# One kernel, another sequence of its work list: logits of the first unit first, unit 2 ahead of the queries, the first projection ahead of a mixing product

## The chip, the cores and the metric

The kernel runs on 1 core of one Trainium2 chip. The metric is the device time of one execution in microseconds; lower is better. The core has five engines with queues of their own: PE (TensorE, matrix products), DVE (VectorE), ACT (ScalarE), POOL (GpSimd) and SP, which here only issues DMA transfers. Each engine runs its own instructions strictly in the order in which the program lists them and waits for semaphores of the others.

## The reference

Four tensors q, k, v and f_logit of shape (4, 8, 768, 48) go through a gated linear recurrence, and its result through a Fourier mixing layer with a two-layer network (768 tokens, 384 channels, 1536 hidden channels):

```python
f = 1.0 / (1.0 + np.exp(-f_logit))
for t in range(S):
    state = f[:, :, t, :, None] * state + np.einsum('bhd,bhe->bhde', k[:, :, t], v[:, :, t])
    y[:, :, t] = np.einsum('bhd,bhde->bhe', q[:, :, t], state)
# x: y as (4, 768, 384)
X = np.fft.fft(np.fft.fft(x, axis=1), axis=2)
u = x + np.real(X)
un = (u - mean(u)) / np.sqrt(var(u) + 1e-06)
return u + np.maximum(un @ w_ch1, 0.0) @ w_ch2
```

## The kernel before, in words

The recurrence is cut into 16 **units**: unit u is batch u // 4 and a pair of heads (u % 4). A unit's channels lie on the partitions and its 768 tokens along the free axis, in six chunks of 128 tokens. The Fourier layer is a product with tables over tokens and one over channels, done per batch once its four units are there. The network is done per batch in three pairs of 128-token blocks.

Each unit is a Python generator (`attention` and `outputs`), and one `next` runs it to its next `yield`. A batch has three more generators: `fnet` (the Fourier products), `turns` (normalising and transposing for the network) and `projected` (the network). What runs when is written out by hand in one string, `ORDER`, of 970 words. Each word makes one step, and the loop behind it at line 1074 and following records the instructions of that step at once. So the sequence of the words is the sequence on every engine. There is no scheduler behind it. A word `L2fk` issues the loads of logits and keys of unit 2 on SP, a bare number such as `2` runs the next step of unit 2, `K2` transposes its weighted keys, `F0`, `H0`, `P0` step the three generators of batch 0, `r` loads a block of network weights (they come in 64-bit words) and `C` converts a loaded block to 32 bits, `I` sets constants, `i` loads the identity matrix, `E` prepares the triangle of ones for the running sums, `Z` clears buffers.

The lines that the steps below speak of:

- Line 411 (ACT) takes exp(-logits) in place. For the four units of batch 0, PE then transposes it by chunks into PSUM (423, tiles `pg`), ACT takes the logarithm out of PSUM (425, into `early`), PE forms the running sums with the triangle (433, `run`), and ACT makes the two weights out of them (439, 440) and the ends (441). For later units DVE does the running sums with a scan (449) instead.
- Lines 462 and 464 (DVE) multiply queries and keys by the weights, in place. 472 (PE, `sc`) forms the token-by-token products, 476 (DVE) copies the allowed half to SBUF (`at`), 610 (PE, `st`) transposes the weighted keys, 631 and 648 (PE) form the outputs and the second half of the products, 673 (PE, `ds`) the state increments, 681 (DVE, `stt`) scans the states, 690 (PE) adds their share to the output.
- Lines 319, 321, 322, 323 convert a block of weights (ACT, DVE twice, POOL).
- Line 824 (PE, `mix`) is the channel product of the Fourier layer, 883 (DVE) adds its result to x, 865 (PE, `pt`) transposes normalised rows, 959 (PE, `up`) is the first layer of the network for the first two block pairs. Later pairs use a scheme with 15 products instead of 24 whose sums DVE makes (899) for PE (927).
- PSUM: the tiles named `run`, `sc`, `st`, `ds`, `yt` share two buffers in turn, the tiles `pg`, `z`, `mix`, `pt`, `up` share two others. A step that takes a buffer waits until its earlier content has been read.
- The program gives SP's transfers eight semaphores in turn, so a further one is issued when the one eight places before it has landed. A load into a buffer also waits for the last reader of what lay there; the keys of units 0 and 3 share one buffer (`k_87` in the lists below).

Of the kernel before, what the change touches and what calls it, by code (L numbers as in the profile page):

```python
# [12 lines left out]
C = 128  # L13
# [11 lines left out]


ORDER = (
# [27 lines left out]
)  # L55


# [1162 lines left out]
```

## Time and profile before

| what | us |
|---|---|
| median of three runs | 508.57 (508.08 to 509.59) |
| the profiled execution's own time | 512.57 |
| its span, first to last instruction | 510.8 |
| PE busy in the span | 485.5 (95%) |
| DVE busy | 363.8 (71%) |
| ACT busy | 233.1 (46%) |
| POOL busy | 89.5 (18%) |
| mean granted clock of PE | 0.993 |

Busy time of PE counts a matrix product from its start to its modelled end. Products overlap, so a busy PE need not be at its peak. In a timeline row, the first number is the start in us from the start of the span, the second the duration, and the bracket at the end says how long the engine sat idle before and what ended that. The profiled execution took 4.0 us more than the median of the unprofiled runs.

### The profile page before, as it was taken

The page shows a single profiled execution, that of the slowest core. Times are in us where ns is not written, and L with a number is a line of the kernel's source. Part 1 is how long each engine was busy: PE and PEld are TensorE (multiplying, and loading weights), DVE is VectorE, ACT ScalarE, POOL GpSimd, SP SyncE. Part 2 cuts the span into 40 slices and gives each one's busy share as a digit, 9 for nine tenths or more (in the row PEclk, how much of TensorE's full clock was granted, in tenths as well). Part 3 has the DMA queues.
Part 4 walks back from the last instruction along what each step waited for, and adds up shares of the span by engine and source line. Part 5 has one row for each costly group of instructions (what it writes and reads, how often), then busy time and mean ns, then how long its engine had stood idle before and what let it go on. Part 6 is the DMA issues. An engine that isn't in the chain of part 4 may idle for free.

```text
span 510.8 us, 13829 instructions
## 1 busy us (share of the span) xinstructions
PE 485.5 (95%) x5806; PEld 450.2 (88%) x5806; DVE 363.8 (71%) x711; ACT 233.1 (46%) x552; POOL 89.5 (18%) x136
## 2 busy tenths in 40 slices
PE   4878889999999999999999999999999999999997
PEld 4766677886798999998998989999999999999997
DVE  2489988999959684585777886777486666558653
ACT  4688678866230541446463554452431413232130
POOL 2126632644222100000031000111000000010100
PEclk9799999999999999999999999999999999999999
DMA  8877946555201101113011112121200331134001
GB/s 225 236 210 192 248 144 206 170 174 155 83 1 47 38 3 37 43 54 103 30 48 37 49 43 59 58 57 41 98 1 15 110 124 63 62 138 143 31 3 38
DMA packets 20075, 46.20 MB, mean 90 GB/s; under 512 B 3489, under 2 KB 6242, under 8 KB 20002
## 3 DMA queue, kind: packets, MB, share of 16 engines
q1 hardware_dynamic: 18898, 41.66, 28.0%
q0 software_dynamic: 1104, 3.54, 1.9%
q8 instruction: 48, 0.79, 0.7%
q14 instruction: 25, 0.20, 0.1%
HBM read 40.47 MB, written 4.72 MB: 88 GB/s over the span
## 4 chain that ended last, share of the span: by engine, by line
PE 87%; DVE 4%; DMA 3%; ACT 2%; issue 2%; POOL 1%; SPq 0%; POOLq 0%; DVEq 0%; ACTq 0%
PE ub L927 26%; PE fx L982 17%; PE fz L982 12%; PE up L959 6%; PE y L631 3%; PE z L804 3%; PE po L968 3%; PE mix L824 2%; PE y L690 2%; PE ds L673 2%; PE sc L472 2%; PE pt L865 2%; DMA raw<-in_w_ch_dram 2%; PE yt L711 1%; PE run L433 1%
## 5 line engine op out<-in xcount | busy, mean ns | idle before, releaser
L936 DVE TENSOR_TENSOR h<-h,ub 128x512 f32<-128x512 f32 x90 | 61.0, 686 | 32.4 <-PE ub L927 24.7
L934 ACT ACTIVATE h<-ub 128x512 f32<-128x512 f32 x60 | 35.6, 593 | 51.9 <-PE ub L927 50.6
L772 POOL DMA_INDIRECT out_dram<-x,place x16 | 21.3, 1332 | 179.8 <-DVE x L1040 124.3
L927 PE MATMUL ub<-wide,w 128*128 128x128 f32 x400 | 49.8, 276 | 1.7 <-DVE wide L899 1.7
L927 PEld LDWEIGHTS ub<-wide,w 128*128 128x128 f32 x400 | 47.3, 192 | 2.4 <-DVE wide L899 1.6
L939 ACT ACTIVATE h<-h 128x512 f32<-128x512 f32 x50 | 31.1, 632 | 35.2 <-DVE h L936 35.2
L982 PE MATMUL fx<-block,h 128*128 128x192 f32 x264 | 46.7, 327 | 0.0
L982 PE MATMUL fx<-w,h 128*128 128x192 f32 x264 | 45.6, 328 | 0.0
L982 PEld LDWEIGHTS fx<-block,h 128*128 128x128 f32 x264 | 43.4, 190 | 0.2
L982 PEld LDWEIGHTS fx<-w,h 128*128 128x128 f32 x264 | 42.6, 190 | 0.2
L927 PE MATMUL ub<-unT,w 128*128 128x128 f32 x320 | 41.0, 275 | 0.0
L927 PEld LDWEIGHTS ub<-unT,w 128*128 128x128 f32 x320 | 38.4, 192 | 0.0
L323 POOL TENSOR_TENSOR w<-w,raw 128x384 uint32<-128x384 uint32 x24 | 27.7, 1161 | 56.7 <-ACT raw L319 18.7
L959 PE MATMUL up<-unT,w 128*128 128x256 f32 x144 | 33.2, 384 | 0.1
L927 PE MATMUL ub<-wide 128*128 128x128 f32 x240 | 31.9, 276 | 0.9 <-DVE wide L899 0.9
L927 PE MATMUL ub<-unT,wide 128*128 128x128 f32 x240 | 32.2, 277 | 0.0
L866 ACT COPY unT<-pt 128x384 f32<-128x384 f32 x24 | 11.4, 476 | 42.2 <-PE pt L865 42.0
L959 PEld LDWEIGHTS up<-unT,w 128*128 128x128 f32 x144 | 26.7, 190 | 4.3 <-DVE x L887 0.4
L927 PEld LDWEIGHTS ub<-wide 128*128 128x128 f32 x240 | 29.4, 192 | 1.2 <-PE ub L927 1.1
L927 PEld LDWEIGHTS ub<-unT,wide 128*128 128x128 f32 x240 | 29.2, 192 | 0.4
L982 PE MATMUL fz<-block,h 128*128 128x192 f32 x132 | 23.5, 328 | 0.0
L476 DVE COPY_PREDICATED at<-causal,sc 128x768 f32<-128x768 uint32 x16 | 16.6, 1040 | 9.3 <-PE sc L472 8.0
(216 smaller groups left out, 1011.4 us busy)
## 6 DMA issues: line engine op xcount, KB each, us to landing
raw<-in_w_ch_dram SPq DMA_DIRECT2D x24, 384.0 KB, 5.1
v<-in_v_dram SPq DMA_DIRECT2D x16, 288.0 KB, 3.8
k<-in_w_ch_dram SPq DMA_DIRECT2D x12, 384.0 KB, 3.6
g<-in_w_ch_dram SPq DMA_DIRECT2D x12, 384.0 KB, 4.1
k<-in_qkf_dram SPq DMA_DIRECT2D x25, 144.0 KB, 3.4
g<-in_qkf_dram SPq DMA_DIRECT2D x20, 144.0 KB, 4.6
q<-in_qkf_dram SPq DMA_DIRECT2D x20, 144.0 KB
wide<-in_qkf_dram SPq DMA_DIRECT2D x11, 144.0 KB, 4.3
```

What stands on the lines that cost most here:

```text
L323: nc.gpsimd.tensor_tensor(bits, bits, lo, ALU.add)
L476: nc.vector.copy_predicated(AT, causal[:, :64].bitcast(U32).unsqueeze(1).unsqueeze(1).to_broadcast([128, 2, NCH, 64]), own[:, :, :NCH * 64 ...
L631: nc.tensor.matmul(y[FILL[g], c // 3, c % 3 * C + t.start:c % 3 * C + t.stop], lhsT=vals[rows, o:o + (64 if g == 0 else D)], rhs=weights, ...
L772: nc.gpsimd.indirect_dma_start(out=out.rearrange("b s d -> (b s) d"), out_offset=bass.IndirectOffsetOnAxis(ap=place[:, b, i:i + 1], axis=0 ...
L804: nc.tensor.matmul(z[:, cols], lhsT=src[:, j, lo:hi], rhs=tab[:, t, T % 2, cols], start=(i == 0), stop=(i == len(parts) - 1), skip_group_c ...
L927: nc.tensor.matmul(chains[chain][:, m * 128:(m + 1) * 128], lhsT=block(w)[:, m * 128:(m + 1) * 128], rhs=tokens(a), start=(new and m == 0) ...
L934: nc.scalar.activation(out, got, kind, scale=1.0 if how == "=+" else -1.0)
L936: nc.vector.tensor_tensor(out, out, got, ALU.add if how == "+" else ALU.subtract)
L939: nc.scalar.activation(out, out, AF.Relu)
L959: nc.tensor.matmul(pp[:, :256], lhsT=w1[:, kt, m * 128:(m + 1) * 128], rhs=unT[:, kt], start=(kt == 0), stop=(kt == 2))
L968: nc.tensor.matmul(po[:, :DM], lhsT=h[:, m, t], rhs=w2[:, m], start=(m == 0), stop=(m == NF - 1))
L982: nc.tensor.matmul(out, lhsT=h[:, m], rhs=blocks[i][:, m], start=(start and m == 0), stop=(m == H - 1), skip_group_check=True)
```

## The change

Only the string `ORDER` differs. Both hold the same 970 words, each the same number of times, so the same instructions are recorded, in another sequence. (Where buffers are handed out in turn, the tile numbers differ.) The start of the diff:

```diff
 ORDER = (
-    "I L1f L0f i L0v E 1 0 0 1 0 0 L0k r C 0 1 1 0 L0q 0 0 1 L2f 2 L1q 0 Z 0 K0 0 0 r 2 2 r 1 L1k 1 L3fk "
-    "L2q 0 0 2 1 0 0 1 3 1 L2k C C 2 L1v 0 3 3 K1 L4fk 0 1 0 2 L3q 3 1 1 1 2 2 4 1 0 1 3 3 3 L3v 1 2 3 2 "
+    "Z E L0f 0 L1f 1 i L2f r L0q L0v L0k 0 L2k 2 I 1 r 0 0 C 0 2 1 1 0 0 0 1 L1q 1 0 2 0 K0 0 2 L3fk 1 "
+    "L1k 0 0 0 3 1 2 0 K1 3 3 L2q 0 0 2 1 L3v 2 1 L1v C 1 1 L4fk L3q 0 2 0 0 0 3 1 1 1 3 3 3 L2v 3 1 4 2 "
...
```

The rest of the string differs all along, by small moves: the first `P0` stands at place 216 instead of 220, units 8 and 9 change places for a while, the last 31 words are `P3` in both.

**First place: the loads at the start, on SP.** `g_85`, `k_87`, `q_89` and `v` are logits, keys, queries and values of unit 0, `g_86` and `q_90` logits and queries of unit 1, `raw` a block of weights; the first `wide` is the logits of unit 2. Before:

```order
L250 DMA g_86<-in_qkf_dram 96x768
L251 DMA g_86<-in_qkf_dram 16x768
L250 DMA g_85<-in_qkf_dram 96x768
L251 DMA g_85<-in_qkf_dram 16x768
L1112 DMA ident<-in_ident_dram 128x128
L233 DMA v_141<-in_v_dram 128x576
L234 DMA vx_142<-in_v_dram 64x288
L244 DMA k_87<-in_qkf_dram 48x768
L246 DMA k_87<-in_qkf_dram 32x768
L248 DMA k_87<-in_qkf_dram 16x768
L348 DMA raw_176<-in_w_ch_dram 128x768
L250 DMA q_89<-in_qkf_dram 96x768
```

Now:

```order
L250 DMA g_85<-in_qkf_dram 96x768
L251 DMA g_85<-in_qkf_dram 16x768
L250 DMA g_86<-in_qkf_dram 96x768
L251 DMA g_86<-in_qkf_dram 16x768
L1112 DMA ident<-in_ident_dram 128x128
L250 DMA wide<-in_qkf_dram 96x768
L251 DMA wide<-in_qkf_dram 16x768
L348 DMA raw_144<-in_w_ch_dram 128x768
L250 DMA q_89<-in_qkf_dram 96x768
L251 DMA q_89<-in_qkf_dram 16x768
L233 DMA v_148<-in_v_dram 128x576
L234 DMA vx_149<-in_v_dram 64x288
```

The logits of unit 0 are loaded ahead of those of unit 1, and those of unit 2 follow at once; values and keys of unit 0 come later. Further on, the keys of unit 1 stand behind the keys of units 2 and 3, where they stood ahead of both.

**Second place: DVE around units 1 and 2.** `q_90`, `g_86` are unit 1's, `stt_351` and `stt_355` unit 0's states, `at_92` unit 1's products, `wide` in lines 462 and 464 is unit 2's. Before:

```order
L462 TENSOR_TENSOR q_90<-q_90,g_86 112x768
L464 TENSOR_TENSOR g_86<-W_202,k_88 112x768
L681 SCALAR_TENSOR_TENSOR stt_351<-ds_332,te_98 112x288
L476 COPY_PREDICATED at_92<-causal,sc_0_363 128x768
L321 TENSOR_SCALAR w_107<-raw_282 128x384
L322 SCALAR_TENSOR_TENSOR w_107<-raw_282,w_107 128x384
L321 TENSOR_SCALAR w_107<-raw_294 128x384
L322 SCALAR_TENSOR_TENSOR w_107<-raw_294,w_107 128x384
L462 TENSOR_TENSOR wide<-wide 112x768
L464 TENSOR_TENSOR wide<-W_401,wide 112x768
```

Now:

```order
L462 TENSOR_TENSOR q_90<-q_90,g_86 112x768
L464 TENSOR_TENSOR g_86<-W_227,k_88 112x768
L681 SCALAR_TENSOR_TENSOR stt_355<-ds_338,te_98 112x288
L462 TENSOR_TENSOR wide<-wide 112x768
L476 COPY_PREDICATED at_92<-causal,sc_0_394 128x768
L321 TENSOR_SCALAR w_107<-raw_186 128x384
L322 SCALAR_TENSOR_TENSOR w_107<-raw_186,w_107 128x384
L464 TENSOR_TENSOR wide<-W_351,wide 112x768
```

The query product of unit 2 stands ahead of the copy of unit 1, and one of the two weight conversions there is made later. Ahead of the first line 883 DVE now has 6 conversions, where it had 7; between the first and the second line 883 it has 3 conversions, where it had 2, and a copy (476) that stood there now comes behind.

**Third place: PE at the first projection.** `pt_3` is the transposition that completes its input, `yt` and `y` belong to outputs of units of batch 1, `mix_2` the third mixing product of batch 0. Before:

```order
L865 MATMUL pt_3_1447<-ident,un_3_1397 128x128 x3
L711 MATMUL yt_1460<-ident,yT_1240 128x112 x6
L690 MATMUL y<-wide,stt_1445 48x128 x10
L824 MATMUL mix_2_1477<-cd,zz_1081 128x193 x2
L824 MATMUL mix_2_1477<-cd,zz_1081 128x192 x2
L959 MATMUL up_0_0_1499<-unT_0_1309,w_107 128x256 x3
```

Now:

```order
L865 MATMUL pt_3_1407<-ident,un_3_1368 128x128 x3
L472 MATMUL sc_0_1432<-wide 64x64 x24
L690 MATMUL y<-wide,stt_1416 48x128 x10
L711 MATMUL yt_1479<-ident,yT_1214 128x112 x6
L959 MATMUL up_0_0_1487<-unT_0_1307,w_107 128x256 x3
L824 MATMUL mix_2_1492<-cd,zz_1092 128x193 x2
```

The first projection stands ahead of the third mixing product, no longer behind it.

50 rows, old and new, of the table ORDER are left out of this document.

## The prediction

> **What bounds the kernel now.** I read the page first, for the engine that ends last.
>
> ```profile
> PE 485.5 (95%) x5806; PEld 450.2 (88%) x5806; DVE 363.8 (71%) x711; ACT 233.1 (46%) x552; POOL 89.5 (18%) x136
> ...
> PE   4878889999999999999999999999999999999997
> ...
> PE 87%; DVE 4%; DMA 3%; ACT 2%; issue 2%; POOL 1%; SPq 0%; POOLq 0%; DVEq 0%; ACTq 0%
> ```
>
> PE is the bound: 95% busy, 87% of the chain that ended last, and its slices are full from the eighth on. Since both lists hold the same instructions, PE's work is the same. The time can only move by PE's idle time (510.8 - 485.5 = 25.3 us) and by the rate at which PE runs. Where does the idle time lie? Busy time by stretches of 10 us (PE, PEld, DVE, ACT, POOL, then PE's granted clock, DMA share, GB/s):
>
> ```profile
> 0.00:10.00 10.00, 2.81 (x14) 2.58 (x15) 2.09 (x3) 4.58 (x8) 2.96 (x21) 1.00 0.78 216
> 10.00:20.00 10.00, 8.54 (x128) 7.64 (x127) 5.67 (x7) 6.75 (x13) 3.29 (x12) 0.84 1.04 264
> 20.00:30.00 10.00, 9.48 (x218) 8.30 (x216) 3.77 (x6) 7.89 (x22) 0.98 (x1) 0.82 0.80 219
> 30.00:40.00 10.00, 7.77 (x307) 7.00 (x297) 9.35 (x11) 7.62 (x19) 1.86 (x3) 1.00 0.70 199
> 40.00:50.00 10.00, 7.72 (x237) 6.42 (x230) 9.78 (x17) 8.22 (x20) 6.71 (x12) 1.00 0.70 196
> 50.00:60.00 10.00, 8.41 (x238) 6.81 (x230) 9.44 (x20) 6.54 (x20) 8.75 (x15) 1.00 0.85 219
> 60.00:70.00 10.00, 7.80 (x163) 6.02 (x162) 8.99 (x13) 7.60 (x22) 2.79 (x3) 1.00 0.81 236
> 70.00:80.00 10.00, 8.71 (x224) 7.34 (x225) 8.54 (x19) 8.00 (x26) 2.97 (x3) 1.00 0.52 166
> 80.00:90.00 10.00, 9.54 (x196) 7.71 (x187) 8.53 (x21) 8.46 (x24) 3.74 (x4) 1.00 0.57 175
> 90.00:100.00 10.00, 10.00 (x121) 8.55 (x118) 9.66 (x13) 8.66 (x23) 6.69 (x6) 1.00 0.60 176
> ```
>
> Up to 90 us PE idles 90 - 70.8 = 19.2 us. So 6.1 us are left behind that. From 30 to 60 us DVE is the fullest engine (28.6 of 30 us) and PE waits on it. Up to 30 us DVE has 18.5 us to spare, because it waits for the first loads, logarithms and products. So there are three regimes: a start set by loads and a chain across engines, a middle set by DVE, and from the first projections (85 us) on a PE that always has work. Who ends PE's waits, over the whole span (us in total, times, longest):
>
> ```profile
> PE pg L423 <- ACT g L411: 7.2, 1, 7.2
> PE y L690 <- DVE stt L681: 4.7, 6, 1.3
> PE ub L927 <- DVE wide L899: 2.6, 4, 0.9
> ```
>
> The first is the start, the second the middle, the third all that DVE costs PE in the late stage.
>
> **The change, part by part.** The start, in order of time:
>
> ```profile
> 4.25 0.84 ACT L411 ACTIVATE g<-g 112x768 f32<-112x768 f32 x1 [2.15 <-DMA g<-in_qkf_dram]
> ...
> 4.99 0.19 ACT L411 ACTIVATION_READ_ACCUMULATOR g<-g 112x1 f32 x1
> ...
> 6.20 0.84 ACT L411 ACTIVATE g<-g 112x768 f32<-112x768 f32 x1 [1.01 <-DMA g<-in_qkf_dram]
> ...
> 7.18 2.28 PE L423 MATMUL pg<-ident,g 112*128 112x112 f32 x10 [7.18 <-ACT g L411]
> ...
> 10.89 0.65 ACT L319 ACTIVATE raw<-raw,two 128x384 f32<-128x384 uint32 x1 [1.04 <-DMA raw<-in_w_ch_dram]
> ...
> 12.12 0.90 ACT L439 ACTIVATE g<-run,rise 112x768 f32<-112x768 f32 x1 [0.57 <-PE run L433]
> ...
> 13.05 0.96 DVE L462 TENSOR_TENSOR q<-q,g 112x768 f32<-112x768 f32 x1 [1.27 <-ACT g L439]
> ...
> 14.20 0.96 DVE L464 TENSOR_TENSOR g<-W,k 112x768 f32<-112x768 f32 x1 [0.19 <-DVE q L462]
> ...
> 15.19 0.31 SPq L244 DMA_DIRECT2D k<-in_qkf_dram  x1
> ...
> 16.32 1.04 DVE L476 COPY_PREDICATED at<-causal,sc 128x768 f32<-128x768 uint32 x1 [1.16 <-PE sc L472]
> ...
> 16.90 1.20 PE L610 MATMUL st<-ident,g 112*128 112x112 f32 x5 [0.71 <-ACT deep L441]
> ...
> 18.64 0.96 DVE L464 TENSOR_TENSOR g<-W,k 112x768 f32<-112x768 f32 x1 [0.45 <-DMA k<-in_qkf_dram]
> ...
> 23.78 0.76 DVE L681 TENSOR_TENSOR_SCAN stt<-ds,te 112x288 f32<-112x288 f32 x1 [4.18 <-PE ds L673]
> ...
> 25.32 0.90 ACT L439 ACTIVATE wide<-run,rise 112x768 f32<-112x768 f32 x1 [1.72 <-PE run L433]
> ```
>
> *The first logits.* PE's first products need unit 0's exponentials, which came second (6.20 + 0.84, PE at 7.18). Loaded first they are made at 4.25. PE then waits for the identity, 64 KB behind both pairs of logits, which were there at 6.20.
>
> For landings I use a line through two rows. The first weight block, behind 1768 KB in the old list (by the shapes in the list, itself included), was there at 10.89. Unit 1's keys, behind 3832 KB, were there at 18.64. So 2064 KB took 7.75 us, 0.375 us per 100 KB. The identity lands at about 6.4, and PE starts 0.8 us sooner.
>
> *What takes this gain away.* ACT now also has unit 2's exponential (0.84 + 0.19) between the logarithms, so line 439 of unit 0 starts at about 11.4, not 12.12. Unit 0's keys stand behind 2440 KB, where 1384 KB were, and land at 10.89 + 672 x 0.00375 = 13.4. So line 464 starts at 13.4, 0.8 us sooner, and the copy 476 of unit 0 likewise. But the transposition at line 610 waits for a buffer that unit 1's line 441 frees (0.71 us in the row at 16.90), and unit 1's lines 439 to 441 now stand behind one more logarithm of unit 2 on ACT. I put them where they were. The 0.8 us end there: nil at 17 us.
>
> *Unit 2's running sums* go ahead of unit 0's remaining outputs on PE, so that its line 439 comes well ahead of 25.32. Six of these products delay unit 0's state increments, and the scan at 23.78 moves later. Against that, the increments no longer stand behind other transpositions of unit 2. I take +0.4 us (bounds 0 and +1.5).
>
> *DVE's middle.* The rows that carry it:
>
> ```profile
> 26.91 1.04 DVE L476 COPY_PREDICATED at<-causal,sc 128x768 f32<-128x768 uint32 x1 [2.37 <-PE sc L472]
> 27.84 0.35 DVE L321 TENSOR_SCALAR w<-raw 128x384 uint32<-128x384 uint32 x1
> 28.23 0.56 DVE L322 SCALAR_TENSOR_TENSOR w<-raw,w 128x384 uint32<-128x384 uint32 x1
> ...
> 30.38 0.95 DVE L462 TENSOR_TENSOR wide<-wide 112x768 f32<-112x768 f32 x1
> ...
> 74.52 0.54 DVE L883 TENSOR_TENSOR x<-mix,x 128x384 f32<-128x384 f32 x1
> ```
>
> Ahead of the copy at 26.91 DVE idles 2.37 us, and from there to 74.52 it hardly idles at all. Unit 2's query product (0.95 us at 30.38) now goes into that idle time. It needs unit 2's queries, behind 4696 KB: 18.64 + 864 x 0.00375 = 21.9, early enough. That is -0.95 us. One weight conversion fewer stands ahead of the first line 883: 0.35 + 0.56 = -0.9 us. With +0.4 from the scan, line 883 comes at 74.52 - 1.45, about 73.1. Bounds: 0 if PE, not DVE, holds the middle, and -2.9 if the scan is not late and a second conversion's worth of idle goes.
>
> *The first projection.* Between the first and second line 883 a conversion more (+0.9) and a copy less (-1.04) nearly cancel. PE's order there has the third mixing product behind the projection:
>
> ```profile
> 75.60 1.49 PE L824 MATMUL mix<-cd,zz 97*128 97x193 f32 x8
> ...
> 84.97 1.56 PE L959 MATMUL up<-unT,w 128*128 128x256 f32 x6
> ```
>
> So the first projection comes at 84.97 - 1.5 - 1.5 = 82.0. Only one of these 1.5 us is a gain: the mixing product is done later instead, at its full 1.5. The postponed conversion falls where PE is 10.00 of 10 busy and DVE 9.66, so projections cover it. Without that cover it would cost 0.9.
>
> *The late stage* is shuffled too, by small moves. Its price is PE's wait for DVE's sums, 2.6 us in four pieces now. I see no reason for a sign and take 0, with bounds -2.6 (all gone) and +2.6 (doubled).
>
> **Sum.** -1.5 us: 512.57 becomes 511.1 for a profiled execution, its span 510.8 becomes 509.3. The median shown lies 4.0 below the profiled time, so 508.57 becomes **507.1**.
>
> **The rivals.**
>
> *The gain ends in a wait.* The opening gain already ends in the wait at 610. If PE's own chain (its six waits on line 681 are 4.7 us) holds the middle, fewer DVE instructions help nothing: 508.6, no change. For it: PE waits on one unit's scan. Against it: DVE at 9.78 of 10.
>
> *Unit 1's keys come late (slower).* They now stand behind the keys of units 2 and 3: 4360 KB instead of 3832, so 20.6 by the line. Worse, unit 3's keys go into unit 0's buffer, and their issue waits for line 464 of unit 0, as the row at 15.19 shows (14.20 + 0.96). Unit 1's keys are stuck behind it on SP. DVE takes its work in order, so line 464 of unit 1 holds unit 0's scan behind it. It costs nothing until it would end after about 24.2, that is with keys landing after 23.2. If each of these loads waits its turn they could land at 27: 3.8 us late, less the 1.5 gained, 510.9.
>
> *The clock.* Rows by stretch and of one product at two rates:
>
> ```profile
> 16.80:23.60 6.80, 6.70 (x127) 5.75 (x127) 2.35 (x3) 5.02 (x12) 0.00 (x0) 0.50 0.90 220
> ...
> 21.48 0.88 PE L631 MATMUL y<-at,v 64*48 64x64 f32 x24
> ...
> 31.94 0.55 PE L631 MATMUL y<-at,v 64*48 64x64 f32 x24
> ```
>
> For 6.8 us PE is granted half its clock, and the same 24 products take 0.88 instead of 0.55. At full clock 6.7 us of work would be 4.2. If the denser start keeps the clock up, up to 2.5 us more go: 504.6. I give it little, as PE was busy 8.54 of 10 us in the stretch in which the clock fell.
>
> The Trainium skill ("TensorE: Matmul & The Clock Gate", Part 1: The HAM clock gate) says that the clock is halved by default, released after a busy window of about 3.4 us and halved again only after an idle one, in windows that run freely. By that rule a start at 6.4 would stay released, and the sum would be that of this rival. The trace does not agree: the half clock at 16.8 follows no idle time over 0.71 us.
>
> *PE fills better.* In the new list a `sc` product of unit 5 stands ahead of unit 4's outputs, and PE idles 9.6 us between 30 and 80. A fifth of that less, on top of the forecast, is 505.2.
>
> **How the numbers follow.** About 0.3% (1.5 us) is what a measurement of this kernel can tell from no change, so "faster" means under 507.0 and "slower" over 510.1. The forecast, 507.1 with its own range 505.8 to 508.6, gets 0.45, of which 0.24 under 507.0. Gain lost gets 0.16. Late keys get 0.18, together with a late stage that waits more (508.57 - 1.5 + 2.6 = 509.7 at a doubling, more if it is worse). The clock gets 0.11, the fuller PE 0.10. Faster 0.24 + 0.21 = 0.45, same 0.21 + 0.16 = 0.37, slower 0.18. The range 504.2 to 510.6 takes in the clock at one end and nearly all of late keys at the other.
>
> **What would show it.** In the changed profile: PE's first line 423 at about 6.4, not 7.18. Line 439 of unit 0 at 11.4, not 12.12. The query product of unit 2 must start before the copy 476 of unit 1. Line 464 of unit 1 at 20.6 to 21 with a wait on a load. The first line 883 at about 73.1 and the first line 959 at about 82. PE idle up to 90 us near 17.7 instead of 19.2, and behind 90 us near 6.1. I am wrong if line 464 of unit 1 starts after 23.2, if line 883 has not moved, or if the waits of line 927 grow past 4 us. A stretch near 17 us with a clock above 0.50 would be the clock rival.

## The result, and the profile after

| | before | new list |
|---|---|---|
| median, 20 executions each | 510.29 us (508.08 to 515.29) | 514.91 us (510.82 to 519.50) |
| ratio, 95% interval | | 1.0073 (1.0048 to 1.0099) |
| profiled execution, its span | 512.57, 510.8 | 514.33, 512.5 |

The new list is 0.7% slower. The forecast was 507.1. (The ratio is taken over executions within 1.5% of the fastest of their kernel, for the new list 17 of 20, while the medians are of all 20. The three times that were shown of before, 508.1 to 509.6, were short ones: 101 executions of it in the experiments below have a median of 510.98.) The page of the new list, PE's busy time and the clock that it was granted, by fortieths of the span:

```profile
PE 485.3 (95%) x5806; PEld 449.8 (88%) x5806; DVE 361.9 (71%) x711; ACT 232.7 (45%) x552; POOL 88.0 (17%) x136
...
PEclk9998899999999999999999999999999999999999
```

PE is as busy as before (485.5). But the slices with less clock have moved: one at the second place before, now two at the fourth and fifth. Busy time by stretches of 10 us (PE, PEld, DVE, ACT, POOL, then PE's clock, DMA share, GB/s), where the new list loses:

```profile
30.00:40.00 10.00, 6.26 (x283) 5.59 (x277) 7.22 (x11) 9.26 (x20) 3.22 (x9) 0.98 0.99 231
40.00:50.00 10.00, 8.32 (x199) 6.73 (x196) 8.64 (x14) 5.59 (x16) 4.19 (x4) 0.85 0.66 182
50.00:60.00 10.00, 6.58 (x244) 5.63 (x236) 9.76 (x18) 7.29 (x18) 9.04 (x18) 1.00 1.00 254
60.00:70.00 10.00, 9.85 (x158) 7.00 (x159) 8.75 (x14) 7.06 (x21) 3.25 (x3) 0.83 0.29 93
```

From 30 to 40 us PE is busy 6.26 us, where it was 7.77, and from 50 to 60 us 6.58, where it was 8.41; and behind each of these the clock is lower. PE's waits over the whole span (us in total, times, longest):

```profile
PE st L610 <- DVE at L476: 2.4, 2, 1.9
PE y L690 <- DVE stt L681: 2.2, 3, 1.0
PE up L959 <- ACT h L961: 2.1, 2, 1.3
PE sc L472 <- issue: 1.9, 1, 1.9
PE ub L927 <- DVE wide L899: 1.9, 3, 0.6
```

The wait for the scans (681) fell from 4.7 to 2.2 us, as wished. In its place stand three others: for a copy (476), for ACT in the projections (959), and a pause inside a run of line 472 in which PE waits for nothing that the profile shows ("issue"). On PE in order of time (start, duration, in the bracket the idle time before it):

```profile
22.61 0.67 PE L610 MATMUL st<-ident,g 112*128 112x112 f32 x5 [0.68 <-DVE g L464]
...
39.08 0.28 PE L472 MATMUL sc<-wide 48*64 48x64 f32 x3 [1.89 <-issue]
...
59.15 0.70 PE L610 MATMUL st<-ident,g 112*128 112x112 f32 x5 [1.92 <-DVE at L476]
...
95.49 1.56 PE L959 MATMUL up<-unT,w 128*128 128x256 f32 x6 [1.30 <-ACT h L961]
```

Now the stretches of half clock, where the granted clock is 0.50, and the 3.41 us ahead of each (same columns). New list:

```profile
36.22:39.64 3.42, 1.53 (x97) 1.39 (x92) 1.54 (x4) 3.36 (x7) 1.68 (x6) 1.00 0.96 212
39.64:43.05 3.41, 3.41 (x62) 2.77 (x52) 2.09 (x4) 0.74 (x1) 1.11 (x1) 0.50 0.61 170
56.70:60.12 3.42, 1.22 (x21) 0.82 (x16) 3.32 (x8) 2.39 (x5) 3.09 (x9) 1.00 0.96 283
60.12:63.53 3.41, 3.38 (x24) 2.25 (x25) 3.38 (x4) 1.43 (x6) 1.70 (x2) 0.50 0.79 254
```

Before:

```profile
13.40:16.81 3.41, 2.04 (x56) 1.53 (x54) 2.06 (x3) 3.02 (x8) 1.82 (x11) 1.00 1.03 302
16.81:23.64 6.83, 6.74 (x127) 5.75 (x127) 2.34 (x3) 5.01 (x12) 0.00 (x0) 0.50 0.90 221
```

Each half-clock stretch is 3.41 us long or twice that, and behind a stretch of 3.41 us in which PE was busy 0.45, 0.36 and (before) 0.60 of the time. In the rest of both profiles, from the first product on, no stretch of this grid is under 0.63, and none is followed by half clock unless it was at half clock already. (Up to 12.3 us in the new list and 13.4 us before, the trace has no record of the clock, and the rows print 1.00 there. But the products of line 423 take 394 ns each up to 11.8 us in the new list, as in the half-clock stretch of before, 392, and 259 ns at full clock. So both lists start at half clock.) A wait of 1.9 us thus cost twice here: its own length, and about 1.7 us in the next 3.4 us. The Trainium skill ("TensorE: Matmul & The Clock Gate", Part 1: The HAM clock gate) gives such a window as 3413 ns, running freely against the kernel; the trace agrees. It sets half clock behind an idle window; here a window that was busy for over a third was enough.

In the two profiled executions half clock lasts 6.8 us in both, so their spans differ by only 1.7 us. Over all executions it does not. Each execution has its mean clock on record, and (1 - clock) x span is what half clock cost it directly, at most. (Some of it costs nothing: in the profile of the old front with the new late stage, below, all of it, 0.9 us, lies behind PE's last product.) Means by clock, over the executions of before in the experiments (107, one of 1719 us left out) and of the new list (20):

| mean clock of the execution | before: executions, mean us | new list: executions, mean us |
|---|---|---|
| 0.999 and over | 44, 509.6 | none |
| 0.996 to 0.998 | 27, 511.9 | 1, 510.8 |
| 0.992 to 0.995 | 27, 512.7 | 5, 513.8 |
| 0.988 to 0.991 | 5, 515.1 | 6, 515.0 |
| under 0.988 | 4, 516.9 | 8, 517.6 |

At the same clock the two lists take the same time within about 1 us. But two thirds of the executions of before are at 0.996 or more, and 1 in 20 of the new list. Over the 101 executions of before and the 17 of the new list that are compared here and below, (1 - clock) x span is 1.6 us before and 5.2 us now, on average, and what is left of the span is 507.8 and 507.9.

### The profile page after: what moved, and what is told of

The parts are those of the page before. It is cut to its first block, busy times and chain, and to the rows that moved or that the text cites. A ratio compares the mean times of both kernels' runs of the same rounds, so it can differ in the third digit from the quotient of the medians.

```text
span 512.5 us, 13813 instructions
## 1 busy us (share of the span) xinstructions
PE 485.3 (95%) x5806; PEld 449.8 (88%) x5806; DVE 361.9 (71%) x711; ACT 232.7 (45%) x552; POOL 88.0 (17%) x136
## 4 chain that ended last, share of the span: by engine, by line
PE 83%; DVE 7%; DMA 5%; ACT 3%; issue 2%; SPq 0%; POOL 0%; DVEq 0%; POOLq 0%; ACTq 0%
PE ub L927 26%; PE fx L982 17%; PE fz L982 12%; PE z L804 4%; PE up L959 4%; PE po L968 3%; PE y L631 3%; PE mix L824 3%; DMA g<-in_qkf_dram 2%; PE y L690 2%; PE ds L673 2%; PE pt L865 1%; PE sc L472 1%; DMA v<-in_v_dram 1%; PE yt L711 1%
## 5 line engine op out<-in xcount | busy, mean ns | idle before, releaser
L936 DVE TENSOR_TENSOR h<-h,ub 128x512 f32<-128x512 f32 x90 | 61.2, 685 | 35.1 <-PE ub L927 24.1
L772 POOL DMA_INDIRECT out_dram<-x,place x16 | 16.2, 1012 | 214.0 <-DVE x L1040 127.7
L323 POOL TENSOR_TENSOR w<-w,raw 128x384 uint32<-128x384 uint32 x24 | 31.3, 1308 | 61.0 <-DVE w L322 24.4
L866 ACT COPY unT<-pt 128x384 f32<-128x384 f32 x24 | 11.4, 474 | 29.0 <-PE pt L865 29.0
L982 PE MATMUL fz<-w,s 128*128 128x192 f32 x132 | 23.5, 328 | 0.0
L982 PE MATMUL fz<-block,h 128*128 128x192 f32 x132 | 23.4, 327 | 0.0
```

The source lines that it names most:

```text
L323: nc.gpsimd.tensor_tensor(bits, bits, lo, ALU.add)
L772: nc.gpsimd.indirect_dma_start(out=out.rearrange("b s d -> (b s) d"), out_offset=bass.IndirectOffsetOnAxis(ap=place[:, b, i:i + 1], axis=0 ...
L936: nc.vector.tensor_tensor(out, out, got, ALU.add if how == "+" else ALU.subtract)
L982: nc.tensor.matmul(out, lhsT=h[:, m], rhs=blocks[i][:, m], start=(start and m == 0), stop=(m == H - 1), skip_group_check=True)
```

## The experiments

All kernels are orders of the same 970 words, and some add words of their own. "Half clock" in the table is the mean of (1 - clock) x span over the executions compared. The median of before, measured beside them, was 510.7 to 511.4 us. The ratios with their intervals are as recorded and can differ from the quotient of two medians: for 1.0093 that quotient is 1.0134.

| kernel | median us | ratio to before, 95% | half clock, us |
|---|---|---|---|
| before (101 executions) | 510.98 | | 1.6 |
| new list | 514.91 | 1.0073 (1.0048 to 1.0099) | 5.2 |
| new to word 88, then old | 512.83 | 1.0046 (1.0006 to 1.0086) | 2.4 |
| new to word 171, then old | 515.02 | 1.0060 (1.0029 to 1.0092) | 5.1 |
| new to word 419, then old | 517.54 | 1.0093 (1.0058 to 1.0129) | 6.9 |
| old to 86, new to 171, then old | 511.54 | 1.0020 (0.9990 to 1.0050) | 4.4 |
| old to 419, then new | 509.95 | 0.9982 (0.9956 to 1.0009) | 1.1 |
| new opening repaired, then old, from 419 new | 511.20 | 1.0027 (1.0003 to 1.0052) | 1.8 |

**Where the loss lies.** A list's first words can be joined to the other list's remaining ones, in the order in which they stand there. At word 419 both lists have done exactly the same words; at 88 and 171 all but two.

```diff
 ORDER = (
-    old[:419] + old[419:]
+    new[:419] + (old without the words done)      # likewise with 88 and 171
```

The new front:

> The first 419 words of the new list (up to about 165 us), then the old list's remaining words: at that place both lists have done exactly the same words. If the time was lost in the front (the start, the middle, the first projections): near the new list or a little above it, since the old late stage idles 0.7 us more on line 899: 514.5 to 515.7, ratio to before 1.007 to 1.010. If it was lost in the late stage: near before, 510.3, ratio 0.998 to 1.002.

Measured 1.0093, the slowest of all the joined lists: the loss is in the front, and more than the whole of it. (The profiled execution of this kernel took 1586 us and is not read.)

The opening alone:

> The first 88 words of the new list (the start up to unit 2's second half of products, about 36 us), then the old list's remaining words. Forecast of step one of the prediction (the opening is a gain, and was lost later): copy 476 of unit 1 at 25.5 as in the new list, against 26.9, no half clock at 16.8 to 23.6, and 1.4 to 3 us less in the end: 507.5 to 509. Rival (the denser opening itself brings the loss: PE runs ahead and stands still at 37 us for want of instructions, then falls to half clock): a pause of 1 to 2 us in PE around 36 to 39 us inside a run of line 472, a half clock behind it, and 511 to 514 in the end.

1.0046, not faster. In its profile the copy 476 of unit 1 came at 27.72, behind a wait of 2.12 us ahead of line 610 at 21.2 and a stretch at half clock from 24.1 to 27.5. The forecast gain of the opening is refuted. The rival's time came, but not by its path: the pause inside line 472 of unit 3 was 0.66 us here, and no half clock followed it.

Up to word 171:

> The first 171 words of the new list (up to about 70 us in its profile), then the old list's remaining words. The first 88 alone gave 1.0046 times the time before, with 2.4 us of it by half clock. If the middle (words 88 to 171: the pause at 37 us, the copy of unit 5 behind the sums over unit 3 at 57 us) brings the rest of the loss by half clock: mean clock 0.988 to 0.991, time 514 to 515.5. If the first projections (words 171 to 300, PE idle 2.1 us at 94 and 104 us) bring it: as with 88 words, 512 to 513, clock 0.995.

1.0060 with 5.1 us of half clock, as the first theory said: with the new middle behind the new opening, the half clock is there.

The new middle behind the old opening:

> The old list's first 86 words, then the new list's words up to 171, then the rest of the old. So the old opening with the new middle. With the new opening and middle it was 1.006, with the new opening alone 1.0046, and 5.1 and 2.4 us of it by half clock, against 1.6 to 2.1 before. If the middle does it by itself: 1.003 to 1.006, half clock costing 4 to 5 us. If it needs the state that the new opening leaves (later states, loads that bunch up around 30 to 38 us): 0.999 to 1.002, half clock 2 us.

The ratio, 1.002, is that of the second theory and the half clock, 4.4 us, that of the first. By these two numbers the new middle waits less and loses the clock more. Its profile, with PE's share first and the clock third from the end:

```profile
45.23:48.64 3.41, 1.71 (x71) 1.47 (x68) 3.34 (x7) 2.50 (x6) 3.01 (x5) 1.00 0.55 143
48.64:55.47 6.83, 6.28 (x155) 5.76 (x155) 6.66 (x13) 4.03 (x12) 6.51 (x12) 0.50 1.05 221
```

Busy 0.50, then half clock for two windows, although 6.28 of these 6.83 us were busy. Its five executions between 0.992 and 0.995 take 511.1 us on average, where those of before take 512.7.

The new late stage behind the old front:

> The first 419 words of the old list, then the new list's remaining words. In the profiles this boundary lay at 181.9 us in the old list and at 184.7 in the new, and the ends at 507.0 and 508.7: so the new late stage is 1.0 us shorter. If that holds: 509.5 against 510.6 before, ratio 0.996 to 1.0, clock as before (0.997). If the late stages are equal or the front's state carries over: 510.6 or more.

Its median is 1.0 us below that of before beside it, as expected, though the interval still holds no change. This is the best of the lists run, and the only one with a median under before's.

**Does a wait bring the half clock?** In the late stage PE has work without a break. Eleven waits of four lengths were put there:

```diff
+    def gap(n):
+        far = [t.rearrange("p r c n -> p (r c n)")[:, :512] for t in at_t]
+        nc.tensor.matmul(spare, lhsT=ident, rhs=ident, start=True, stop=True, ...)
+        nc.scalar.copy(far[0][:, :128], spare)
+        for i in range(n):
+            nc.scalar.copy(far[(i + 1) % 2], far[i % 2])
+        nc.tensor.matmul(spare, lhsT=far[n % 2][:, :128], rhs=ident, start=True, stop=True, ...)
```

> The old list, with eleven waits of four lengths put into PE's work where it is full (between 361 and 500 us): a product of constants, its copy by ACT out of PSUM, none to three further copies of 128 x 512 by ACT, and a product of what they made, which PE must wait for. Estimated waits, by ACT's copies of this size in the profile (0.5 us) and 0.4 for the way there and back: 0.8, 1.4, 2.0 and 2.6 us, 18 us in all. Results are not touched. Theory waits: each costs its own length, 528 us, and the clock stays at 0.996. Theory clock: a stretch of 3.4 us in which PE was busy less than 0.6 of the time is followed by half clock in the next one. Waits of 0.8 never do it, those of 2.0 and 2.6 mostly, those of 1.4 now and then (by where they fall), so some 6 stretches at half clock, 1.7 us each, on top: 538 us, clock about 0.977.

Median 539.7 us, clock 0.981 to 0.990 in its four executions. The time is near that of the clock theory and the clock lies between the two, but the waits came out longer than estimated, 0.4 to 4.7 us and 20.5 us together, so the time alone does not decide. On average (1 - clock) x span is 7.0 us, where it was 2.0 in the executions of before beside it. Three of the eleven waits were followed by half clock in the profile, where six were expected. Windows of the grid with a wait, and the one behind each:

```profile
369.19:372.60 3.41, 1.18 (x10) 1.18 (x11) 1.72 (x6) 1.95 (x6) 0.00 (x0) 1.00 0.00 0
372.60:376.02 3.42, 3.42 (x18) 3.42 (x18) 1.38 (x2) 0.63 (x1) 0.00 (x0) 0.51 0.00 0
...
403.39:406.81 3.42, 0.96 (x8) 0.77 (x8) 1.63 (x7) 2.50 (x5) 0.97 (x1) 0.99 0.16 58
406.81:410.22 3.41, 3.41 (x18) 3.41 (x17) 0.88 (x3) 1.14 (x2) 0.00 (x0) 0.50 0.16 58
437.52:440.94 3.42, 1.71 (x15) 1.71 (x16) 0.29 (x1) 1.92 (x5) 0.00 (x0) 1.00 0.05 17
440.94:444.35 3.41, 3.41 (x33) 3.41 (x32) 1.99 (x6) 1.50 (x3) 0.00 (x0) 1.00 0.00 0
468.24:471.65 3.41, 1.83 (x13) 1.61 (x12) 1.94 (x7) 1.74 (x4) 0.97 (x1) 1.00 0.18 62
471.65:475.07 3.42, 1.95 (x17) 1.95 (x18) 0.49 (x2) 1.88 (x4) 0.97 (x1) 1.00 0.16 58
475.07:478.48 3.41, 3.41 (x33) 3.41 (x33) 3.13 (x9) 1.26 (x3) 0.00 (x0) 1.00 0.36 111
```

A wait of 2.31 us that fell into one window (share 0.35) was followed by half clock, one of 2.46 us (0.28) too, and so was the longest, 4.71 us, which left a whole window empty. A wait of 3.05 us at 470.07 that fell across two windows (0.54 and 0.57) did not, nor one of 1.75 us (0.50). So the waits do it: only they, and the few instructions that make them, were added there. It is the busy share of a window rather than the length of the wait that counts, and where a wait falls against the windows is chance. Here, among long dense products, the bound lies between 0.35 and 0.50. Among the short products of the first 60 us it is higher and not sharp. In all profiles with clock records 26 windows at full clock were followed by half clock, and the fullest of them was busy 0.64 (all waits filled, below, at 43.5 us). But windows of 0.50, 0.55 and 0.58 were followed by full clock (this kernel at 10.8 us, the old front with the new late stage at 11.4, and the same with fill, below, at 12.0). What else decides between 0.50 and 0.64 is not shown. The price, by the rows of the same products:

```profile
371.42 0.49 PE L229 MATMUL y<-ident,at 128*128 128x128 f32 x2 [2.31 <-ACT at L228]
371.75 4.47 PE L935 MATMUL ub<-wide,w 128*128 128x128 f32 x24
376.05 1.06 PE L935 MATMUL ub<-unT,wide 128*128 128x128 f32 x8
```

(Line 935 is line 927 of the other kernels.) Eight products take 1.06 us and each further eight 0.89 at full clock (0.89 between their starts in the rows of before), 24 thus 2.8; here 4.47, which is 1.6 us more.

**Filling the waits.** Small products of constants, placed where PE waits:

```diff
-    ... "4" (L673 of unit 4) "5" ...
+    ... "4" D D D "5" ...          # D: 8 products of 128x128 bf16, their sums not read
```

> The new list with 24 small products of constants (into an unused part of a PSUM bank, never read) on PE where it idles 1.92 us ahead of line 610 of unit 5. The wait stays as long as it was; PE is only not idle in it. Theory clock (PE's rate is halved for 3.4 us behind a stretch of 3.4 us in which PE was too little busy): the half clock at 60.1 to 63.5 is gone, and the time is 1 to 1.7 us below the new list: 513.2 to 514, with a mean granted clock higher by about 0.003. Theory waits (only the lengths of the waits count): as the new list, 514.9, half clock where it was.

516.62 us, ratio 1.0070 (1.0030 to 1.0111). (The outputs of this kernel are not the reference's, so that only its time and rows are read; why they differ is not shown.) In its profile they run for 1.51 us in the wait, and no half clock follows there. But the half clock of this kernel, 4.3 us on average against 5.2, is hardly lower, and the time is not: other windows were low in its executions. All waits at once:

> The new list with small products of constants on PE (8 at a time, some 0.5 us, 112 in all, their sums never read) in ten of the waits that its profile shows between 15 and 105 us: ahead of line 610 of units 0, 1 and 5, line 631 of units 1 and 2, line 690 of units 1 and 3, line 711 of unit 1, and two of line 959. The waits are left as they are; PE is only not idle in them. Theory clock: the time that half clock costs, (1 - clock) x span, falls from 5.7 us to about 2, mean clock 0.996, and the time is 511 to 512, ratio to before 1.001 to 1.003. Theory waits: nothing changes, or the products are in the way: 515 to 517, clock 0.989.

The half clock fell to 2.1 us, as the clock theory said, but the time was 518.52 us, ratio 1.0111 (1.0055 to 1.0166). So filling returns the clock and costs more than that. Why, shows the same trial on the best list:

> The old list up to word 419 and the new list's late stage, with small products of constants (8 at a time, 72 in all) in seven of the waits that the old list's profile shows: ahead of line 610 of unit 0, line 690 of units 1, 3, 4 and 5, line 631 of unit 2, line 711 of unit 2 or 3. Theory clock: what half clock still costs the old front (1.6 us on average, up to 6 in single executions) falls to 0.5, mean clock 0.999, and the times spread less: 508.7 to 509.5 against 510.7 before, ratio 0.995 to 0.998. Theory waits: as without the products, 509.95, ratio 0.998.

513.89 us, ratio 1.0040 (1.0008 to 1.0072), against 0.9982 without the products. PE's waits in its profile from 10 to 110 us:

```profile
PE sc L472 <- issue: 1.2, 1, 1.2
PE run L433 <- issue: 0.9, 1, 0.9
PE mix L824 <- issue: 0.6, 1, 0.6
```

2.7 us of pauses for which nothing is to be seen, where the list without the products has none in these 100 us. The products are instructions too, and PE has to be given them (below); that this is why they cost time is argued, not shown. So the fill is no clean trial of the clock, and the inserted waits above are a cleaner one.

**Repairs, one wait at a time.** The copy of unit 5 stood on DVE behind the sums over unit 3 (lines 739 to 747, 55.1 to 58.2 us). This kernel puts it and the scan of unit 4 ahead of most of those sums, and unit 5's outputs ahead of line 804:

```diff
-    ... 3 3 4 4 5 3 4 3 S 7 7 K5 6 4 4 L7qv F0 5 ...
+    ... 3 5 4 4 4 3 3 3 S 7 7 K5 6 4 4 L7qv 5 F0 ...
```

> The new list with four words moved: DVE makes the copy 476 of unit 5 and the scan 681 of unit 4 ahead of its share of the Fourier layer's sums over unit 3 (lines 742 to 761), and PE forms unit 5's first outputs ahead of the first product 804 at 61.6 us. Theory waits: PE's wait of 1.92 us ahead of line 610 of unit 5 falls under 0.4, but line 804 cannot start before its tables at 61 us, so 0.9 us are gained, not 1.9: 514.0. Theory clock: in addition the stretch from 56.7 to 60.1 has PE busy 0.64 instead of 0.36 and the half clock behind it goes: 512.3 to 513. If neither matters: 514.9.

517.93 us, ratio 1.0101 (1.0047 to 1.0154). The wait of 1.92 us is gone and 1.41 us stand two steps further on, ahead of line 631 of unit 5, which waits for ACT's reading of unit 4's outputs (704). The wait moved.

The keys of unit 1 sooner:

```diff
-    ... K0 0 2 L3fk 1 L1k 0 ...
+    ... K0 0 2 L1k L3fk 1 0 ...
```

> The new list with one word moved: the keys of unit 1 are loaded ahead of the logits and keys of unit 3, no longer behind them. Line 464 of unit 1, which waited 3.81 us for them and ran at 21.50, should run near 18. Theory clock (each stretch of 3.4 us with PE busy under about 0.6 costs half the clock in the next one, some 1.7 us; the runs differ by which stretches fall so): the stretch from 19 to 24 us, in which PE waits ahead of line 610 for the scan behind that line 464, is full again, the mean granted clock rises from 0.989 to about 0.993, and the time is 512 to 513.5. Theory waits (only PE's own idle time counts): 0.7 us, 514.2, clock as it was.

515.60 us, 1.0104 (1.0074 to 1.0134). Line 464 of unit 1 ran at 17.77 without a wait, as expected. PE still waited, 0.85 us, at the same line 610, now for the scan 681 itself (21.80, behind the increments 673), and 0.61 us for instructions. So the late keys were not what held it.

A block of weights later:

```diff
-    ... 1 r 2 4 1 L4qv 2 4 L5qv K3 3 T C 3 L6fk 4 2 1 3 4 L7fk 5 1 ...
+    ... 1 2 4 1 L4qv 2 4 L5qv r K3 3 T 3 L6fk 4 2 1 3 4 L7fk 5 C 1 ...
```

> The new list with the fourth block of weights loaded some 10 us later, and converted 4 us later, so that 393 KB fewer are under way between 30 and 38 us, where the DMA engines are full (1.0 of the time). Theory loads (PE pauses inside line 472 of unit 3 because its next 16 KB of instructions arrive late, and they arrive late because the DMA engines are full): the pause of 1.89 us at 37.2 falls under 0.7, the half clock behind it goes, and the time is 512 to 513.5. Rival (PE uses up its instructions in a dense run of short products, whatever else is loaded): the pause stays at 1.5 us or more, and the time is 514 to 515.

The pause inside line 472 of unit 3 is 0.45 us, not 1.89, as the load theory said; the time, 514.88 us (1.0101, 1.0063 to 1.0139), is that of the rival. Two stretches at half clock came elsewhere (23.4 and 50.7 us). All repairs and some fill:

> The new list with all three repairs: the keys of unit 1 sooner, the fourth block of weights later, and small products of constants on PE in two of its waits (8 ahead of line 610 of unit 0, 24 ahead of line 610 of unit 5), which change no result. Theory clock: no stretch of 3.4 us under 0.6 is left but by chance, so the time that half clock costs falls from 5.7 us to 1 to 2.5 us, mean clock 0.995 to 0.998, and the time is 510 to 511.5, near the kernel before. Theory waits: 2 us gained at 21 and 37 us, 513, clock as in the new list.

513.85 us, 1.0073 (1.0046 to 1.0101), half clock 4.7 us. Neither theory's number: taking single waits away moves the low windows, it does not lift the middle above the bound.

**The opening.** Two words of it put back, between the old rest and the new late stage:

```diff
-    ... K0 0 2 L3fk 1 L1k 0 0 0 3 1 2 0 K1 3 3 ...
+    ... K0 0 2 L1k L3fk 1 0 0 0 3 1 2 0 3 3 K1 ...
```

> The new list's first 88 words with two words moved (keys of unit 1 ahead of the logits and keys of unit 3; the transposition of unit 1's keys, which waits for the scan of unit 0, behind the transpositions of unit 3's logarithms, as in the old list), then the old list up to word 419, then the new late stage. It is to be compared with the old front and the new late stage: 0.998. If the new opening lost by these two waits: 0.993 to 0.997, copy 476 of unit 1 near 25 us, no half clock between 20 and 30 us. If the new opening costs for another reason (unit 2's sums ahead of unit 0's outputs, loads): 1.0 to 1.004, with half clock between 20 and 30 us.

1.0027, and in its profile no half clock between 20 and 30 us, so it is the second theory's time without its half clock. This and the old front with the same late stage were both profiled at full clock from 12 us to their last 2 us, and so they show the two openings side by side. DVE with the old opening:

```profile
18.64 0.96 DVE L464 TENSOR_TENSOR g<-W,k 112x768 f32<-112x768 f32 x1 [0.83 <-DMA k<-in_qkf_dram]
20.48 0.76 DVE L681 TENSOR_TENSOR_SCAN stt<-ds,te 112x288 f32<-112x288 f32 x1 [0.88 <-PE ds L673]
23.90 1.02 DVE L476 COPY_PREDICATED at<-causal,sc 128x768 f32<-128x768 uint32 x1 [2.66 <-PE sc L472]
```

With the new one, repaired:

```profile
18.41 0.96 DVE L464 TENSOR_TENSOR g<-W,k 112x768 f32<-112x768 f32 x1 [0.26 <-DMA k<-in_qkf_dram]
22.72 0.76 DVE L681 TENSOR_TENSOR_SCAN stt<-ds,te 112x288 f32<-112x288 f32 x1 [3.35 <-PE ds L673]
...
25.86 1.03 DVE L476 COPY_PREDICATED at<-causal,sc 128x768 f32<-128x768 uint32 x1 [0.78 <-PE sc L472]
```

PE ahead of the increments that the scan waits for, with the old opening:

```profile
18.00 0.79 PE L423 MATMUL pg<-ident,wide 112*128 112x112 f32 x6
...
19.58 0.85 PE L673 MATMUL ds<-v,kT 128*64 128x48 f32 x20
```

With the new one, repaired:

```profile
18.05 1.56 PE L433 MATMUL run<-early 128*112 128x128 f32 x12
...
20.40 0.76 PE L673 MATMUL ds<-v,kT 128*64 128x48 f32 x17
22.32 0.37 PE L673 MATMUL ds<-v,kT 128*64 128x96 f32 x3 [1.15 <-issue]
```

The keys are there equally early (18.64 and 18.41), but the scan of unit 0 comes 2.2 us later. Twelve products of unit 2's running sums go ahead on PE, where six transpositions did, and the increments start 0.8 us later. Then PE pauses for 1.15 us inside them. This pause is not of one size: in the other profiles with this opening it is none to 1.58 us. PE from 20 to 30 us (same columns as above), with the old opening:

```profile
20.00:30.00 10.00, 9.45 (x238) 8.30 (x233) 6.70 (x8) 9.66 (x23) 2.64 (x2) 1.00 0.81 223
```

With the new one, repaired:

```profile
20.00:30.00 10.00, 7.51 (x198) 6.39 (x188) 5.01 (x8) 7.08 (x18) 1.61 (x1) 1.00 0.89 233
```

That is 1.9 us less work done, at the same clock.

**The projections.** On ACT the exponentials 453 of units 9 and 8 behind two reads 961 each:

```diff
-    ... 7 7 9 P0 P0 P0 9 ...   ... 8 C 8 8 P0 P0 r ...
+    ... 7 7 P0 P0 9 P0 9 ...   ... C P0 P0 8 8 8 r ...
```

> The new list with four words moved: on ACT the exponentials 453 of units 9 and 8, which wait for POOL's depths (450) behind POOL's share of the postponed weight conversions (323), come behind the reads 961 of two projections each, no longer ahead of them. PE idled 1.30 us at 94.2 and 0.80 us at 104.6 ahead of line 959, because 961 had not freed the buffer. If the postponed conversions starve the projections in this way: both waits of line 959 under 0.3 us, 1.5 to 2 us less than the new list, 512.5 to 513.5, ratio 1.003 to 1.006. If PE would only wait elsewhere (line 472 or 690 of the later units): the waits of line 959 go, others of the same length come, 514 to 515, ratio 1.007. The clock in this part is full either way; the half clock of the earlier part (5.7 us) stays.

515.84 us, 1.0089 (1.0058 to 1.0120): PE waits elsewhere. Its waits from 85 to 110 us, where the new list had 2.1 us in two waits of line 959:

```profile
PE y L631 <- ACT ao L652: 1.6, 1, 1.6
PE sc L472 <- issue: 1.3, 1, 1.3
```

So the place of 453 on ACT alone is not what costs the time. What 453 waits for is a candidate. In the new list:

```profile
90.28 2.66 POOL L323 TENSOR_TENSOR w<-w,raw 128x384 uint32<-128x384 uint32 x1 [1.48 <-ACT raw L319]
92.90 0.52 POOL L450 TENSOR_TENSOR deep<-g,W 112x6 f32<-112x6 f32 x1
```

POOL's share of a conversion takes 2.66 us here (1.01 in the one behind it), and unit 9's depths (450) stand behind it. But before had much the same:

```profile
89.27 2.35 POOL L323 TENSOR_TENSOR w<-w,raw 128x384 uint32<-128x384 uint32 x1 [1.84 <-DVE w L322]
91.57 0.33 POOL L450 TENSOR_TENSOR deep<-g,W 112x6 f32<-112x6 f32 x1
```

PE was busy 10.00 of 10 us there. So the long conversion alone does not make PE wait, and the cause of this part stays open.

## Why the prediction was wrong

- **What bounds the kernel**: right that only PE's idle time and its rate can move the time. It was the rate that did.
- **The first logits** came as worked out: line 423 at 6.24 (6.4 forecast), line 439 of unit 0 at 11.14 (11.4), line 464 at 13.22 (13.4). The last is in part luck: it was to wait for the keys, and it waited for line 462 (0.19 us). Nor did the gain end at line 610 of unit 0, which ran at 16.35, where it was 16.90.
- **Unit 1's keys**: line 464 of unit 1 at 21.50 with a wait of 3.81 for its load, just above the 20.6 to 21 forecast, and up to 23.2 in other profiles with this opening. That it "costs nothing until it would end after about 24.2" failed: line 610 of unit 1 transposes the keys that 464 weights, and PE waits 0.5 to 2.1 us for them there. But with the keys in time the loss remained.
- **Unit 2's running sums**, "+0.4 us (bounds 0 and +1.5)", is the term of the sum that was mis-sized in the opening: with equal clock and keys in time it is 2.2 us at the scan, 1.15 of them a pause of PE that nothing in the profile of before shows. The prediction counts six products of the sums ahead of the increments, and there are twelve (1.56 us). I measured it against the scan at 23.78 in the profile of before, and that profile had half clock from 16.8 to 23.6. At full clock the old opening has the scan at 20.48. So the old opening is better at full clock than its page showed, and 44 of 107 executions had a clock of 0.999 or more; this is what the new one has to be set against.
- **DVE's middle**, -0.95 and -0.9 us, may be worth about what was said where it stands alone: behind the old opening five executions at a clock of 0.992 to 0.995 take 1.6 us less than before's. But line 883 had not moved (74.54, it was 74.52), which I had named as a sign that I was wrong.
- **"The postponed conversion falls where PE is 10.00 of 10 busy ..., so projections cover it"** failed. The first line 959 came 1.6 us sooner (83.39), but the last 2.75 us later (149.92, it was 147.17): PE waits 2.1 us for the chain POOL 323, POOL 450, ACT 453. From word 171 to 419 the ratio rises by 0.33%, within the intervals of the two joined lists. Taking away the wait on ACT moved it to other lines, and before had such long conversions too, so this chain as the cause is neither shown nor the only candidate.
- **The late stage**, 0 with bounds -2.6 and +2.6: some -1.0 by its joined list, whose interval still holds no change. PE's waits at line 927 are 1.9 us, where they were 2.6.
- **The clock** is the step that failed. The sum adds up starts on DVE and PE by their lengths and has no term for a lower clock. The prediction names PE's rate as one of the two things that can move the time, but lets it move only to the fast side, as a rival worth up to 2.5 us. The runs show the slow side: (1 - clock) x span rose from 1.6 to 5.2 us, and of the 3.7 us between the means of the compared executions that is 3.6. The forecast gain of 1.5 us is not there either: what is left is 507.8 and 507.9, and PE idled 19.7 us up to 90 us (17.7 forecast, 19.2 before). From 30 to 60 us PE is busy 6.3 to 8.4 of 10 us in both lists. Waits of up to 1.4 us, spread as in the old list, mostly leave each window above the bound; 1.9 us in one piece, or two waits in one window, do so less often. The rule of the Trainium skill that I set aside as disagreeing ("TensorE: Matmul & The Clock Gate", Part 1: The HAM clock gate) has the right window. Read as "a window with too little work" and not "an idle window", as the profiles here show it, it speaks against this change.
- **"Slower"** had 0.18, for late keys together with a late stage that waits more. The keys alone are not the cause, as the repair shows, and the late stage does not wait more. So the rival that would have had the direction right had it for other reasons.

What stays open: the equal remainder at equal clock (507.8 and 507.9) is itself a sum of an opening that is slower by its waits, a middle and a late stage that are faster and projections that are slower. The joined lists and the rows suggest these signs, but with intervals of about 0.3% each piece is known only to about 1.5 us. Which of the low windows costs how much is not shown either: no repair and no fill brought the time back.

## What to carry to other kernels

Where PE is only two thirds busy, do not add up waits by length: look at its busy share in each 3.4 us. Here one stretch under some 0.5 cost another 1.6 us, and which execution gets it is chance, so compare the mean clocks of many executions. Before a time in a profile is taken as the one to beat, look at the clock that was granted there. A wait that is taken away in a chain across four engines mostly stands again one or two steps further on: of five such repairs here none brought the new list measurably below its 1.007.

## What was not expected of the hardware

PE can pause where the profile shows nothing that it waits for, and the trace's DMA records point at its own instructions. Behind the new opening or with the new middle, where such a pause comes in line 472 of unit 3, it falls at the same place, behind the 43rd (once the 44th) of the 48 products: 1.89 us in the new list's profile, 0.45 to 1.33 in five other kernels, none in some, and 3.95 us in this one (the kernel with 24 products in the wait at 57 us):

```profile
42.69 0.38 PE L472 MATMUL sc<-wide 48*64 48x64 f32 x3 [3.95 <-issue]
```

In the new list's DMA records 16 KB of instructions for PE begin to move at 36.30 us, take 1.39, and PE goes on at 39.08. In the kernel with 3.95 us they begin only at 40.23, 1.5 us after PE had stopped, and PE goes on at 42.69. Up to there the data loads had filled the DMA engines (share 1.05 from 28 to 40 us); from 30 to 38 us it was 1.05 in the new list, 0.96 with the weights later (0.45 us of pause) and 0.81 with the old front (none). The repaired opening had 1.04 and 1.33 us. But full DMA engines alone do not do it: the kernel with the inserted waits, whose front is the old list's, had 0.99 and no pause, and the list with the moved exponentials, the same as the new list word for word up to there, had 1.03 and none. So dense runs of short products (48 in 0.9 us) and full DMA engines go together with these pauses; how much each does, and what is chance, is not settled by one profile of each.
